# K and V loads of an attention kernel: 16 KB read descriptors over four partitions instead of one 4 KB read per partition

## The chip, the cores and the metric

The kernel runs on one core of a Trainium2 chip. The metric is the device time of one execution in microseconds (us), as the median of several runs; less is better.

The engines' names are those of the profile: PE is TensorE, DVE is VectorE, ACT is ScalarE, POOL is GpSimd and SP is SyncE. PEld is PE's loading of weights, which overlaps its matmuls.

## The reference

```python
B, Hq, Hkv, Sq, Sk, D = 16, 32, 8, 16, 2048, 128        # bf16 throughout

def reference(q, k, v):
    rep = Hq // Hkv                                     # 4 query heads share a K and a V head
    k = jnp.repeat(k, rep, axis=1)
    v = jnp.repeat(v, rep, axis=1)
    scores = jnp.einsum("bhqd,bhkd->bhqk", q, k) * D ** -0.5
    p = softmax(scores, axis=-1)
    return jnp.einsum("bhqk,bhkd->bhqd", p, v)
```

This is grouped-query attention with few queries and long keys: for each of the 128 pairs of batch and K/V head, 64 query rows (4 heads of 16) meet 2,048 keys of 128 numbers. K and V are 64 MiB each and are read once; q and the output are 2 MiB each.

## The kernel before

**Work and tiles.** A group `g` is one of the 128 pairs of batch and K/V head; two groups make a pair `p`, and there are 64 pairs. One K group is 2,048 rows of 256 bytes, 512 KB in one contiguous piece of memory. It is loaded into a tile `Kn` of 128 partitions, where partition `a` holds the 16 consecutive rows 16a to 16a + 15, 4,096 bytes. V goes into `Vb` in the same form. There are 12 buffers of `Kn` (`NBK`) and 16 of `Vb` (`NBV`).

**Steps of a pair.** PE transposes both K tiles, 128 x 128 at a time, into a staging area in PSUM with three banks (`KT`, line 501); DVE or ACT copies each bank to the tile `KT` (lines 565 and 595). PE multiplies it with the transposed queries to get the scores (`S`, line 513, 8 matmuls with 512 columns). DVE scales and negates them and takes the row minimum (`max`, line 575), ACT takes the exponential with the row sums (`exp`, line 601). PE transposes the result (`PT`, line 529), DVE or ACT copies that too, and PE multiplies it with V (`PV`, line 544, 32 matmuls). DVE divides by the row sums (`recip`, `norm`, lines 569 and 586) into the tile `O`, which is stored.

**Who decides the order.** When the program is built, `build_schedule` lays every operation of PE, DVE, ACT and SP out in time with a table of durations and a model of the DMA rate (`_BW`, `_BW_SLOW`, `_RING_MB`). It fixes the order on each engine and which of DVE and ACT does each copy. On the chip the engines follow these orders and meet at semaphores. The order of SP is a list written by `sp_program`: for step `t` the two K loads of pair `t`, a transposing load of 512 query rows every fourth step (`issue_q`, line 438), the two V loads of pair `t - 3`, and the store of pair `t - 7` (line 462).

**The loads.** All transfers are issued by SP on one hardware queue. A K load (`issue_k`, line 447) first waits until PE has transposed the tile that was in the buffer; a V load (`issue_v`, line 455) waits for the `PV` of the pair that used the buffer. Each is one `dma_start` whose source is seen as 128 rows of 2,048 numbers, so it reads 4,096 bytes for each partition and writes 4,096 bytes to it, on 16 DMA engines. Its semaphore counts 16 when all have landed.

Of the kernel before, what the change touches and what calls it, by code (L numbers as in the profile page):

```python
# [18 lines left out]
DSTORE = 7  # L19
QCH = 512  # L20
QLEAD = 6


_DUR = {
# [14 lines left out]

def sp_program(NP, qch_pairs, dv=DV, dstore=DSTORE, qlead=QLEAD):  # L40
    sp = []
    n_qch = (NP + qch_pairs - 1) // qch_pairs
    q_step = {c: max(0, c * qch_pairs - qlead) for c in range(n_qch)}
    for t in range(NP + max(dv, dstore) + 1):
        if t < NP:
            sp += [("K", 2 * t), ("K", 2 * t + 1)]
        for c in range(n_qch):
            if q_step[c] == t:
                sp.append(("Q", c))
        if 0 <= t - dv < NP:  # L50
            sp += [("V", 2 * (t - dv)), ("V", 2 * (t - dv) + 1)]
        if 0 <= t - dstore < NP:
            sp.append(("ST", t - dstore))
    return sp
# [235 lines left out]
def bass_standalone__gqa_softmax__sampling_kernel(  # L290
# [13 lines left out]
    J = Sk // 128  # L304
# [16 lines left out]
    Kn = [sb(f"Kn{i}", [128, J, 128], BF16) for i in range(NBK)]  # L321
    Vb = [sb(f"Vb{i}", [128, J, 128], BF16) for i in range(NBV)]
# [14 lines left out]
    sem_k = [sem(f"sem_k{i}") for i in range(NBK)]  # L337
    sem_v = [sem(f"sem_v{i}") for i in range(NBV)]
# [17 lines left out]
    for op in pe_prog:  # L356
        if op[0] == "KT":
            _, p, gg = op
            for h in range(2):
                ld = dict(kind="KT", pair=p, gg=gg, half=h, u=len(loads), eng=None, eidx=None)  # L360
                ld["bank"] = ld["u"] % NSTAGE
                loads.append(ld)
                kt_loads[(p, gg, h)] = ld
        elif op[0] == "PT":
            _, p = op
            for h in range(2):
                ld = dict(kind="PT", pair=p, gg=None, half=h, u=len(loads), eng=None, eidx=None)
                ld["bank"] = ld["u"] % NSTAGE
                loads.append(ld)
                pt_loads[(p, h)] = ld  # L370
# [30 lines left out]
    def norm_wait(p):  # L401
        eng, n = norm_idx[p]
        return sem_nm[eng], n
# [17 lines left out]
    def bh(g):  # L421
        return divmod(g, Hkv)
# [4 lines left out]
    with nc.Block() as block:  # L427

        @block.gpsimd
        def _(gp):  # L430
            gp.iota(iota_t[:, :], [[1, 128]], base=0, channel_multiplier=-1).then_inc(sem_id, 1)  # L431
            gp.wait_ge(sem_id, 1)
            gp.tensor_scalar(ident[:, :], iota_t[:, :], 0.0, None, op0=ALU.is_equal).then_inc(sem_id, 1)  # L433

        @block.sync
        def _(sp):
            def issue_q(c):
                sp.dma_start_transpose(QT[:, qch * c:qch * (c + 1)], qf[qch * c:qch * (c + 1), :]).then_inc(sem_q[c], 16)

            def issue_k(g):  # L440
                s = g % NBK
                if g >= NBK:
                    gprev = g - NBK
                    ld = kt_loads[(gprev // 2, gprev % 2, 1)]
                    sp.wait_ge(sem_stage, ld["u"] + 1)
                b, h = bh(g)
                sp.dma_start(Kn[s][:, :, :], k[b, h].rearrange("(a j) d -> a j d", j=J)).then_inc(sem_k[s], 16)

            def issue_v(g):
                s = g % NBV  # L450
                if g >= NBV:
                    gprev = g - NBV
                    sp.wait_ge(sem_pv, gprev // 2 + 1)
                b, h = bh(g)
                sp.dma_start(Vb[s][:, :, :], v[b, h].rearrange("(a j) d -> a j d", j=J)).then_inc(sem_v[s], 16)

            ocnt = [0] * NBO

            def issue_store(p):
                s = p % NBO  # L460
                sp.wait_ge(*norm_wait(p))
                sp.dma_start(of[128 * p:128 * (p + 1), :], Osb[s][:, :]).then_inc(sem_o[s], 16)
                ocnt[s] += 1

            for op in sp_prog:
                kind, x = op
                if kind == "K":
                    issue_k(x)
                elif kind == "V":
                    issue_v(x)  # L470
                elif kind == "Q":
                    issue_q(x)
                else:
                    issue_store(x)
            for s in range(NBO):
                if ocnt[s]:
                    sp.wait_ge(sem_o[s], 16 * ocnt[s])

        @block.tensor
        def _(pe):  # L480
# [8 lines left out]
            for op in pe_prog:  # L489
                if op[0] == "KT":  # L490
                    _, p, gg = op
                    lds = [kt_loads[(p, gg, h)] for h in range(2)]
                    g = grp(p, gg)
# [148 lines left out]
```

## Time and profile before

| | |
|---|---|
| median of 3 runs | 373.71 us (373.55 to 373.78) |
| the profiled execution: its own time is the span that the profile gives | 370.2 us |
| the median above the span | 3.5 us |
| busy: PE, PEld, DVE, ACT | 331.0, 260.2, 323.0, 261.9 us |
| mean granted PE clock | 0.995 of full speed |
| read from memory, written | 134.22 MB, 2.10 MB |
| mean rate over all DMA packets | 376 GB/s |
| K and V loads, median from issue to landing | 12.9 us |

Busy time is what an engine spent in instructions, and one engine's work overlaps another's. "Issue to landing" contains the time in the queue behind earlier loads. In a list of waits, "A <- B: us, times, longest" says that instruction group A stood still until B was done; "issue" there means that the engine waited for nothing that the profile shows. In the chain of work that ended last, each row has its start, its length and what it was. In the DMA row, each digit stands for a fortieth of the span and gives the busy share in tenths (9 is 90% or more).

### The profile page before, as it was taken

Reading aid. Unit: us, or ns where it says so; the run is one execution under the profiler, and the core shown is the slowest. Engines: PE = TensorE matmul, PEld = TensorE weight load, DVE = VectorE, ACT = ScalarE, POOL = GpSimd, SP = SyncE. Lnnn points to the kernel's source line nnn. Section 1 sums busy time; section 2 is a strip of 40 time slices with the busy share of each in tenths; the row PEclk is TensorE's granted clock in tenths of the full one; section 3 lists DMA queues with packets and bytes.
Section 4 is the critical chain, followed back from the end, with each engine's and each line's share of the span. In section 5 each row is a group of like instructions: output and inputs, shape, how many; then the busy total and the mean of one; then the engine's idle time right before and its main releaser. Section 6 shows DMA issues by size and latency. Waiting matters only on the chain.

```text
span 370.2 us, 13021 instructions
## 1 busy us (share of the span) xinstructions
PE 331.0 (89%) x5632; PEld 260.2 (70%) x5632; DVE 323.0 (87%) x500; ACT 261.9 (71%) x269; POOL 1.0 (0%) x6
## 2 busy tenths in 40 slices
PE   4698998998998989999898999989999898999995
PEld 3576876776776767677776777777777676776764
DVE  2589998998998989899898998989899897999984
ACT  1267766895666885867878676795867778679593
POOL 1000000000000000000000000000000000000000
PEclk9899999999999999999999999999999999999999
DMA  7999999999999999999999999999999999999993
GB/s 262 375 408 341 408 352 405 405 345 407 352 407 410 342 408 350 406 409 347 410 347 408 400 350 413 348 410 370 380 410 346 408 350 399 409 410 410 406 410 112
DMA packets 54840, 139.26 MB, mean 376 GB/s; under 512 B 22016, under 2 KB 22016, under 8 KB 54784
## 3 DMA queue, kind: packets, MB, share of 16 engines
q1 hardware_dynamic: 54784, 138.43, 102.3%
q8 instruction: 45, 0.74, 0.8%
q14 instruction: 11, 0.09, 0.1%
HBM read 134.22 MB, written 2.10 MB: 368 GB/s over the span
## 4 chain that ended last, share of the span: by engine, by line
PE 68%; ACT 21%; issue 4%; DMA 4%; DVE 3%
PE ST_ps L501 26%; PE S_ps L513 17%; PE O_ps L544 14%; PE ST_ps L529 11%; ACT KT L595 11%; ACT PT L595 8%; DMA Vb<-in_v_dram 3%; DVE Sneg L575 2%; ACT P L601 1%; DMA Kn<-in_k_dram 1%; DVE KT L565 1%; DVE PT L565 0%; DVE O L586 0%; DVE rrec L569 0%
## 5 line engine op out<-in xcount | busy, mean ns | idle before, releaser
L575 DVE TENSOR_SCALAR_CACHE_REDUCE Sneg<-S_ps 128x2048 f32<-128x2048 f32 x64 | 146.7, 2292 | 18.6 <-PE S_ps L513 15.1
L501 PE MATMUL ST_ps<-ident,Kn 128*128 128x128 bf16 x2048 | 143.6, 223 | 18.6 <-ACT KT L595 8.1
L501 PEld LDWEIGHTS ST_ps<-ident,Kn 128*128 128x128 bf16 x2048 | 119.6, 99 | 45.1 <-issue 26.7
L601 ACT ACTIVATE P<-Sneg,nbias 128x2048 bf16<-128x2048 f32 x64 | 128.3, 2005 | 11.5 <-DVE Sneg L575 11.5
L565 DVE COPY KT<-ST_ps 128x1024 bf16<-128x1024 bf16 x177 | 116.3, 683 | 9.8 <-PE ST_ps L501 7.6
L595 ACT ACTIVATE KT<-ST_ps 128x1024 bf16<-128x1024 bf16 x79 | 77.6, 1022 | 48.4 <-PE ST_ps L501 48.3
L595 ACT ACTIVATE PT<-ST_ps 128x1024 bf16<-128x1024 bf16 x59 | 57.2, 1021 | 42.2 <-PE ST_ps L529 42.2
L529 PE MATMUL ST_ps<-ident,P 128*128 128x128 bf16 x1024 | 71.6, 220 | 7.5 <-ACT KT L595 3.8
L529 PEld LDWEIGHTS ST_ps<-ident,P 128*128 128x128 bf16 x1024 | 58.2, 98 | 25.1 <-issue 11.4
L513 PE MATMUL S_ps<-KT,QT 128*64 128x512 bf16 x512 | 68.4, 388 | 6.6 <-ACT KT L595 4.4
L544 PE MATMUL O_ps<-Vb,PT 128*64 128x128 bf16 x2048 | 69.6, 220 | 4.2 <-issue 1.4
L544 PEld LDWEIGHTS O_ps<-Vb,PT 128*64 128x64 bf16 x2048 | 59.1, 110 | 11.1 <-issue 2.5
L565 DVE COPY PT<-ST_ps 128x1024 bf16<-128x1024 bf16 x69 | 44.3, 683 | 3.4 <-PE ST_ps L529 3.2
L513 PEld LDWEIGHTS S_ps<-KT,QT 128*64 128x64 bf16 x512 | 25.3, 109 | 26.3 <-issue 9.9
L586 DVE TENSOR_SCALAR O<-O_ps,rrec 128x128 bf16<-128x128 f32 x62 | 21.5, 346 | 9.1 <-PE O_ps L544 9.1
L569 DVE RECIPROCAL rrec<-rowsum 128x1 f32<-128x1 f32 x64 | 10.2, 159 | 4.3 <-ACT P L601 4.1
L601 ACT ACTIVATION_READ_ACCUMULATOR P<-Sneg,nbias 128x1 f32 x64 | 12.9, 202 | 0.0
L575 DVE DVE_READ_ACCUMULATOR Sneg<-S_ps 128x1 f32 x64 | 5.3, 83 | 0.0
L601 ACT ACT_TABLE_LOAD x1 | 1.3, 1283 | 0.7 <-PEq L627 0.7
L612 ACT ACTIVATE O<-O_ps,rrec 128x128 bf16<-128x128 f32 x2 | 0.7, 368 | 0.4 <-PE O_ps L544 0.4
L433 POOL TENSOR_SCALAR ident<-iota_t 128x128 bf16<-128x128 int32 x1 | 0.5, 536 | 0.1
L431 POOL IOTA iota_t<- 128x128 int32 x1 | 0.2, 235 | 0.4 <-POOLq L627 0.4
(4 smaller groups left out, 0.4 us busy)
## 6 DMA issues: line engine op xcount, KB each, us to landing
Kn<-in_k_dram SPq DMA_DIRECT2D x128, 512.0 KB, 12.9
Vb<-in_v_dram SPq DMA_DIRECT2D x128, 512.0 KB, 12.9
out_dram<-O SPq DMA_DIRECT2D x64, 32.0 KB, 12.6
QT<-in_q_dram SPq DMA_TRANSPOSE x16, 12.3
```

The lines of the kernel that those rows point to most:

```text
L433: gp.tensor_scalar(ident[:, :], iota_t[:, :], 0.0, None, op0=ALU.is_equal).then_inc(sem_id, 1)
L501: ins = pe.transpose(stage_ap(ld["bank"], t), Kn[s][:, j, :], ident[:, :])
L513: ins = pe.matmul(S_ps[64 * gg:64 * (gg + 1), 512 * c:512 * (c + 1)], QT[:, 128 * p + 64 * gg:128 * p + 64 * (gg + 1)], kt[:, gg, 4 * c:4 ...
L529: ins = pe.transpose(stage_ap(ld["bank"], t), P[p % 2][:, 128 * j:128 * (j + 1)], ident[:, :])
L544: ins = pe.matmul(O_ps[64 * gg:64 * (gg + 1), 0:128], pt[:, j, 64 * gg:64 * (gg + 1)], Vb[g % NBV][:, j, :], start=(j == 0), stop=(j == J ...
L565: dve.tensor_copy(evac_dst(ld), stage_bank_ap(ld["bank"])).then_inc(sem_ev["dve"], 1)
L569: dve.reciprocal(rrec[:, p:p + 1], rowsum[:, p:p + 1]).then_inc(sem_rec, 1)
L575: dve.tensor_scalar(Sneg[kk % 2][:, :], S_ps[:, :], -scale, None, op0=ALU.mult, op1=ALU.min, accum_out=nbias[:, kk:kk + 1],).then_inc(sem_ ...
L586: dve.tensor_scalar(Osb[s_][:, :], O_ps[:, 0:128], rrec[:, p:p + 1], None, op0=ALU.mult).then_inc(sem_nm["dve"], 1)
L595: act.activation(evac_dst(ld), stage_bank_ap(ld["bank"]), ACT.Copy).then_inc(sem_ev["act"], 1)
L601: act.activation(P[kk % 2][:, :], Sneg[kk % 2][:, :], ACT.Exp, bias=nbias[:, kk:kk + 1], scale=-1.0, accum_out=rowsum[:, kk:kk + 1],).then ...
L612: act.activation(Osb[s_][:, :], O_ps[:, 0:128], ACT.Copy, scale=rrec[:, p:p + 1]).then_inc(sem_nm["act"], 1)
```

## The change

Each K and V load is issued through a new function, `load_wide`. It builds the copy instruction by hand, with a source of 32 rows of 16,384 bytes and a destination of 128 partitions of 4,096 bytes. Read in order, both sides run through the same 512 KB, so each read fills four neighbouring partitions with the bytes that they had before. Waits, semaphores, the queue, the order on SP, and all instructions of the other engines stay as they were; so do the planner's numbers, and the loads of q and the stores.

```diff
+NREAD = 32
...
+            def load_wide(dst, src, sem_):
+                n = src.size()
+                read = bass.AP(src.tensor, src.offset, [[n // NREAD, NREAD], [1, n // NREAD]])
+                ins = mybir.InstDMACopy(
+                    name=nc.get_next_instruction_name(), engine=sp.engine, queue="qSPDynamicHW",
+                    ins=[sp.lower_ap_dma(read)[0]],
+                    outs=[sp.lower_ap_dma(dst.rearrange("a j d -> a (j d)"))[0]],
+                    mode="Copy",
+                )
+                sp.add_instruction(ins).then_inc(sem_, 16)
...
-                sp.dma_start(Kn[s][:, :, :], k[b, h].rearrange("(a j) d -> a j d", j=J)).then_inc(sem_k[s], 16)
+                load_wide(Kn[s][:, :, :], k[b, h], sem_k[s])
...
-                sp.dma_start(Vb[s][:, :, :], v[b, h].rearrange("(a j) d -> a j d", j=J)).then_inc(sem_v[s], 16)
+                load_wide(Vb[s][:, :, :], v[b, h], sem_v[s])
```

## The prediction

> **What bounds the kernel now.** I read the page first (sections 1 to 3), then the waits of TensorE (PE), then the chain in order of time, then the DMA packet and landing records, which the views only summarise.
>
> ```profile
> span 370.2 us, 13021 instructions
> PE 331.0 (89%) x5632; PEld 260.2 (70%) x5632; DVE 323.0 (87%) x500; ACT 261.9 (71%) x269; POOL 1.0 (0%) x6
> DMA  7999999999999999999999999999999999999993
> q1 hardware_dynamic: 54784, 138.43, 102.3%
> ```
>
> The reader sees two full resources: PE at 89% (VectorE, DVE, at 87%) and DMA engines that never rest until the loads end. Which one sets the end is told by who waits for whom:
>
> ```profile
> PE ST_ps L501 <- ACT KT L595: 8.1, 27, 0.4
> ...
> PE ST_ps L501 <- DMA Kn<-in_k_dram: 4.5, 1, 4.5
> ...
> PE O_ps L544 <- issue: 1.4, 1, 1.4
> PE O_ps L544 <- DMA Vb<-in_v_dram: 1.0, 1, 1.0
> ```
>
> PE waited for a load twice only: 4.5 us for the first K tile, 1.0 us for one V tile. The rest is compute handing work around in an order that the program fixed. The chain in order of time shows the beat and that one late V:
>
> ```profile
> 0.72 3.61 DMA Kn<-in_k_dram
> 4.47 3.59 PE ST_ps L501 x32
> ...
> 59.16 1.36 issue
> ...
> 108.71 1.76 ACT PT L595 x2
> ...
> 130.75 1.76 ACT PT L595 x2
> ...
> 152.86 1.76 ACT PT L595 x2
> ...
> 285.35 1.76 ACT PT L595 x2
> ```
>
> Compute repeats every 22.08 us for four pairs ((285.35 - 108.71)/8). Loads do not: the last landing of V 55, 63, 71, 79 and 87 (eight tiles, four pairs apart) is at 172.0, 194.8, 217.5, 240.2 and 263.0 us, a beat of 22.75 us. So DMA is 3% slower than compute, and lives on a stock built early. The spare time between a tile's last landing and its first use shrinks accordingly: V 39 4.85 us, V 55 4.55, V 71 3.21, V 87 1.91, V 103 0.22 (at 310 us, the tile that PE waited for); K 114 has 0.44 at 322 us. After the last Q transpose (292 us) the loads catch up again, to 2.54 us for the last V. The stock lasts almost exactly as long as the kernel: compute sets the end, loads are next in line by a fraction of a us.
>
> **The change, part by part.**
>
> 1. Reads. 256 loads of 512 KB: per load 128 reads of 4,096 B become 32 of 16,384 B; the 128 writes of 4,096 B stay. Per DMA engine (16 of them) that is 256 x 8 = 2,048 reads before and 512 after, 1,536 fewer. In the packet records a 256 B packet takes 18 ns, a 4,096 B one 159 ns (medians; 32,768 of them), and the shortest 8,192 B ones 309 ns. The first two give (159 - 18)/3,840 = 0.0367 ns per byte plus 8.6 ns per packet, and this line puts 8,192 B at 309.4 ns, which fits. If the 8.6 ns belong to the read, a 16,384 B read takes 610 ns instead of 4 x 159 = 636, and the saving is 1,536 x 8.6 ns = 13.2 us of DMA time over the run, 4%. The other ends: if the 8.6 ns belong to the write, the saving is 0. And a far row: the 45 packets of 16,384 B that are in the trace (instruction fetches) take 1,072 ns, 1.7 times 636. I do not take that row, because one of them took 991 ns at 364 us, when the load queue was done: its destination sets it, and K and V do not go there. I take the 610, nearest to the 8,192 B row, and keep 0 for the range; the far row gets only a small chance.
>
> The Trainium skill, "DMA: Bandwidth & Descriptors", section "Why small descriptors are slow (HBM only)", gives a fixed overhead of about 3 cycles per packet; at that page's 850 MHz that is an estimate of 3.5 ns, and the saving would be 5.4 us in place of 13.2, 0.34 us per beat. That would leave the DMA beat at 22.41 us, still above compute's, but the stock would last, and the sum below would be the same.
>
> 2. What that saving is worth. Almost nothing of it reaches the end. At 4% the K and V part of the DMA beat (16 loads x 8 packets x 159 ns = 20.35 us for four pairs) falls by 0.83 us, so the DMA beat goes from 22.75 to about 21.9 us, under compute's 22.08. Then no tile is late, and what remains is compute's fixed order. Gained: the stall at 310 us. PE stood 1.00 us there, but only part moved on: two beats of 22.08 put the ACT copy at 291.07 us to 313.15, and it is at 313.61; the copy at 302.16 us to 324.24, and it stands at 324.69. So 0.46 us of delay went into the chain, and 0.46 us is the gain. What was hidden by it: the next late thing is ScalarE (ACT), already PE's releaser in the first row of the waits.
>
> 3. The first tiles. PE starts at 4.47 us, 0.14 after K 0 has landed, and K 1 follows at 5.6 us against a use at 6.0. K 0's first packets take 1.09 us, then each engine moves 8 packets. With two reads of 610 ns in place of eight of 159 the landing is 0.05 us earlier; if a row is written only when its whole 16 KB read is in, it is 610 - 159 = 0.45 us later. I take -0.05, and +0.45 for the range.
>
> 4. Issue. SyncE still issues 256 loads in the same order with the same waits; an unobstructed one takes 0.39 to 0.45 us, longer ones wait for room. A beat holds 16 loads, 4 stores and one Q transpose: 16 x 0.45 + 4 x 0.43 + 4.5 = 13.4 us of 22.08, so an issue could take 0.5 us longer before SyncE became the pace. Fewer reads to describe should not lengthen it. Cost: 0.
>
> 5. Engines. PE, DVE and ACT instructions are unchanged in kind and order: 0.
>
> 6. Instruction fetch shares these engines. PE's program comes in 45 fetches of 16 KB. Three PE pauses (0.59 us before 37.08 us, 0.56 before 51.76, 1.36 before 60.52) sit at multiples of 256 instructions, each 1.4 to 1.5 us after a fetch's packet ended; all three are on the chain. A fetch goes ahead of or behind load packets. Nearest rows: it could gain if the engines idle now and then, at most those 2.5 us; it could lose if it must wait for a 16 KB read rather than a 4 KB one. I take 0, since the bytes ahead of it need not change; the losing side is rival 2.
>
> Sum: 0.46 + 0.05 = 0.51 us less. The profiled execution's own time is its 370.2 us span, and the runs' median of 373.71 us lies 3.5 us above it (work around the span, and the difference between executions). I carry that 3.5 over unchanged: 373.71 - 0.51 = 373.2 us.
>
> **The rivals.**
>
> Rival 1, the change does not speed up the DMA: the write side, still 4,096 B a piece, sets the 159 ns. For it: only writes to SBUF partitions are split here, and the records do not tell which side owns the 8.6 ns. Against it: nothing in the trace. Time 373.7 us (373.3 to 374.2 with the first tile's bounds).
>
> Rival 2, slower: PE's instruction fetch waits behind longer reads. Place: the boundaries every 256 PE instructions. The packet of a fetch now ends between 0.67 and 5.5 us before PE needs it, and PE needs about 1.45 us. Eight fetches have 1.46 us or less, five more less than 1.92. If each fetch comes 610 - 159 = 0.45 us later, the eight cost 0.45 each and the five the rest, 1.2 together: 4.9 us, of which stretches where ACT paces may hide half: 376.2 to 378.6 us. It decides from a delay of about 0.3 us on. For it: the pauses on the chain now. Against it: 44 of 45 fetches end at least 1.1 us ahead although the engines are always full. The Trainium skill, same page, section "SWDGE vs HWDGE vs iDMA", prefers packets up to 4,096 B because a packet is where an engine switches between queues; that speaks against 16 KB reads, and no row here shows how long a fetch would wait behind one.
>
> Rival 3, slower: a 16 KB read that fills four rows moves its bytes more slowly, for instance because the next read is not started before four writes are out. There is no stock to pay from: each 1% on the K and V packets is 3.0 us by 322 us (325.6 us x 322/350 x 1%), less the 0.2 to 0.4 us that is spare. 2 to 4% gives 379 to 385 us; the far row of step 1 would give over 500. For it: no row with unequal sides exists. Against it: the straight line through 8,192 B, and that each engine already takes four neighbouring rows, so the memory is read in the same order.
>
> **How the numbers follow.** The forecast (DMA faster, compute sets the end) 0.55, rival 1 0.17, rival 2 0.13, rival 3 0.15. The forecast's own range is 371.6 to 373.8 us: down to 1.6 us more gain if the early fetch pauses shrink, up to the first-tile bound. The range of 8 in 10 goes from 371.6 to 378.6 us: it takes in rivals 1 and 2 and leaves out rival 3 and a little at the low end. About 0.2% (0.75 us) is what a measurement of this kernel can tell from no change. The forecast itself sits at 0.14%, inside that: half of it falls below 372.96 us, with the early pauses or the first tiles helping. Faster 0.27, same 0.43, slower 0.30.
>
> **What would show it.** Right: packets of 16,384 B near 610 ns or a load's GB/s above 410 in slices without a Q transpose; a DMA row with slices under 9 after the first quarter; the 1.0 us wait of L544 for Vb gone; the PE, DVE and ACT busy sums and the 22.08 us beat unchanged. Wrong: rows "PE ... <- DMA Vb" or "<- DMA Kn" of several us (rival 3); many "issue" waits of PE, at multiples of 256 instructions (rival 2); DMA tenths and the wait at 310 us as before (rival 1). A beat shorter than 22.08 us would show that I took for compute's own order what was load pacing.

## The result and the profile after

The changed kernel takes 375.72 us (median of 4 runs, 375.04 to 376.34) against 373.63 us for the kernel before, run beside it. The ratio is 1.0056 by the medians; the recorded comparison of the runs puts it at 1.007, with a 95% interval of 1.0045 to 1.0095. It is slower by about 2 us, where the forecast was 0.5 us faster. The ratios here and below leave out runs more than 1.5% above the fastest of their kernel (two of ten in e16, one of four in e12, one of twelve in e17), while the medians keep them.

The page of the changed kernel, sections 1 to 3:

```profile
span 374.3 us, 13021 instructions
...
PE 330.1 (88%) x5632; PEld 259.4 (69%) x5632; DVE 322.9 (86%) x500; ACT 261.9 (70%) x269; POOL 1.0 (0%) x6
...
DMA  8999999999999999999999999999999999999991
...
DMA packets 30264, 139.26 MB, mean 372 GB/s; under 512 B 22016, under 2 KB 22016, under 8 KB 22016
...
q1 hardware_dynamic: 30208, 138.43, 100.1%
```

The engines' busy sums are those of before within 1 us, so no engine does more. The change does what it says: the 32,768 packets of 4 KB are gone. But the DMA row is as full as it was, and the mean rate is 372 GB/s where before had this:

```profile
DMA packets 54840, 139.26 MB, mean 376 GB/s; under 512 B 22016, under 2 KB 22016, under 8 KB 54784
```

The DMA did not get faster.

The waits of PE in the same run (waiter, released by, us in total, times, longest):

```profile
PE ST_ps L513 <- ACT KT L607: 8.1, 27, 0.4
...
PE ST_ps L513 <- DMA Kn<-in_k_dram: 4.8, 1, 4.8
...
PE ST_ps L513 <- issue: 2.7, 3, 1.2
PE S_ps L525 <- issue: 2.4, 3, 1.3
PE O_ps L556 <- issue: 1.6, 1, 1.6
...
PE ST_ps L541 <- issue: 0.8, 1, 0.8
```

The 1.0 us wait for V is gone. What grew is "issue": 7.5 us in 8 waits. Before had 2.7 us in 4, the 1.4 us at line 544 and these:

```profile
PE S_ps L513 <- issue: 0.7, 2, 0.6
PE ST_ps L501 <- issue: 0.6, 1, 0.6
```

The chain in order of time shows the first K tile later and four of the pauses:

```profile
0.73 3.98 DMA Kn<-in_k_dram
...
35.48 1.06 issue
...
58.89 1.63 issue
...
106.25 1.17 issue
...
286.72 1.35 issue
```

PE's weight loads of the two traces can be set side by side, one by one, since their order is the same. The difference (after less before) starts at +0.37 us, is -0.67 us at 16 us and -1.0 us at 25 us, and then rises in steps to +4.07 us: +0.46 (37 us), +0.27 (52), +0.27 (61), +0.19 (68), +1.10 (106), +0.72 (261), +0.26 (277), +1.94 (284), +0.73 (308). Some 0.9 us come back on the way, 0.6 of them at 310 us, where before waited for V. (The two traced executions lie 4.1 us apart; the medians lie 2.1 us apart.) Each step is at an instruction whose number in PE's queue is 193 modulo 256, within a few: where PE goes over to the next 16 KB of its program. At the pauses, the fetch of that piece had ended 1.3 to 1.5 us earlier.

### The profile page after: what moved, and what is told of

It reads as the page before. It is cut to its first block, busy times and chain, and to the rows that moved or that the text cites. A ratio compares the mean times of both kernels' runs of the same rounds, so it can differ in the third digit from the quotient of the medians.

```text
span 374.3 us, 13021 instructions
## 1 busy us (share of the span) xinstructions
PE 330.1 (88%) x5632; PEld 259.4 (69%) x5632; DVE 322.9 (86%) x500; ACT 261.9 (70%) x269; POOL 1.0 (0%) x6
## 4 chain that ended last, share of the span: by engine, by line
PE 69%; ACT 21%; issue 5%; DVE 3%; DMA 1%
PE ST_ps L513 26%; PE S_ps L525 17%; PE O_ps L556 14%; PE ST_ps L541 12%; ACT KT L607 11%; ACT PT L607 9%; DVE Sneg L587 2%; ACT P L613 1%; DMA Kn<-in_k_dram 1%; DVE KT L577 1%; DVE PT L577 0%; DVE O L598 0%
## 5 line engine op out<-in xcount | busy, mean ns | idle before, releaser
L513 PEld LDWEIGHTS ST_ps<-ident,Kn 128*128 128x128 bf16 x2048 | 118.3, 99 | 47.4 <-issue 28.9
L581 DVE RECIPROCAL rrec<-rowsum 128x1 f32<-128x1 f32 x64 | 10.1, 158 | 4.3 <-ACT P L613 4.1
```

Of the source, the lines that this page charges most:

```text
L513: ins = pe.transpose(stage_ap(ld["bank"], t), Kn[s][:, j, :], ident[:, :])
L581: dve.reciprocal(rrec[:, p:p + 1], rowsum[:, p:p + 1]).then_inc(sem_rec, 1)
```

## The experiments

**How the traces are read here.** Three numbers are taken from the packet records and the instructions of each trace. The *wait* of a fetch is the time from PE's crossing of one 256-instruction boundary to the start of the next fetch (44 per run). PE runs through 256 instructions in about 7.5 us, a fetch takes 1.07 us, and PE went on 1.3 to 1.5 us after it, so a wait above about 5 us makes PE pause at the next boundary. A *meeting* is a fetch that takes 2.5 to 2.6 us in place of 1.07 while a Q transpose comes through. And PE's excess over e4, which has neither late fetches nor late tiles (span 366.7 us), is split into what arises in the first 30 us, what arises at fetch boundaries, and the rest, which is mostly late tiles.

**The hand-built copy and the size of the read.** Three kernels differ from the changed one in one number:

```diff
-NREAD = 32
+NREAD = 128        # e1: 4 KB reads;  64 in e2: 8 KB;  16 in e9: 32 KB
```

> The new load function with 128 reads of 4,096 B, so only the hand-built copy instruction is left of the change. Theory A (a fetch of PE's program stands longer behind 16 KB reads) and theory B (a fetch is late only where a Q transpose runs in front of it, and the change moved the Q transposes) both expect the time of before, 373.6 us within 0.5, with PE pauses of kind issue of 2.7 us in sum as in before. Rival C (the hand-built instruction itself is slower to issue or lands later) expects 375 to 376 us as after.

> 64 reads of 8,192 B, each filling two partitions. Theory A expects a third of the loss: 374.0 to 374.8 us, and fetch waits between those of before (3.9 us on average from the crossing of a 256-instruction boundary to the fetch's start) and after (4.1 us). Theory B expects no order by size: anything from 372 to 377 us, with the pauses where a Q transpose lies between crossing and fetch.

> The change with 16 reads of 32 KB per load, each over eight rows (where the two sides of a copy are dealt differently to the engines, rows come to lie in other partitions; then only its time counts). Theory A (fetch waits grow with the read's size): median wait above 4.2 us (3.6 for 4 and 8 KB, 3.9 for 16 KB), late fetches worth 9 us or more, and a time of 376 us or above. Theory B (only where the transposes fall against the fetches counts): median wait 3.9 us or less, and any time from 372 to 377 us.

e1 took 374.28 us against 372.74 (ratio 1.004, interval 1.0023 to 1.0058): a miss of both theories, and short of the 375 to 376 us of rival C. An issue of a load took 0.60 us against 0.43 before (lower quartiles, which leave out the issues that wait for room), but the trace puts the loss elsewhere: one meeting at 31.6 us, after which the last V landed at 366.9 us (364.3 before), and 4.4 us of waits for V:

```profile
PE O_ps L556 <- DMA Vb<-in_v_dram: 4.4, 8, 1.7
PE S_ps L525 <- issue: 0.2, 1, 0.2
```

There were almost no late fetches. e2 took 372.7 us, ratio 1.0005 (0.999 to 1.002): no change, where theory A wanted a third of the loss; its median wait is 3.60 us, that of 4 KB. This pair leaves a rival standing. All seven runs of e1 lie between 373.5 and 374.6 us, so the copy built by hand, without any 16 KB read, already shows 1.5 of the 2.1 us. e2, built in the same way and with the same issue time (0.59 us), shows none. What the copy built by hand adds is thus not told apart from what the size of the reads adds.

e9 took 630.23 us, ratio 1.686 (1.677 to 1.696), far more than anyone expected, and for another reason:

```profile
span 630.3 us, 13021 instructions
...
DMA  9999999999999999999999999999999999999995
...
DMA packets 26168, 139.26 MB, mean 221 GB/s; under 512 B 22016, under 2 KB 22016, under 8 KB 22016
```

Here the DMA engines themselves are slow: 221 GB/s. A 32 KB packet took 2,346 ns (median), 3.7 times a 16 KB one, and already 2,159 ns among the first two loads. So the cost per byte, which is the same from 4 to 16 KB, nearly doubles at 32 KB. The fetch waits (6.1 us) say nothing about theory A, since the whole stream was slow.

**How deep the load queue is.** With 16 KB reads there were 10.1 loads in flight on average, before 8.4. Two kernels limit that:

```diff
+                if kind in ("K", "V"):
+                    if len(recent) >= DEPTH:
+                        sp.wait_ge(*recent[-DEPTH])
+                    recent.append(...)      # the load's semaphore and its count
```

> The change, and SyncE waits before each load until the load issued eight before it has landed, so at most 8 loads are in flight (10.1 on average after, 8.4 before). Theory A expects 375.7 us as after within 0.7, since the reads stay at 16 KB. Theory B in its narrow form (a deeper queue moved the Q transposes) expects the pauses to return to those of before, and 373.2 us within 0.5. The DMA rate per beat should stay at 22.7 us for four pairs.

> Before, with at most 4 loads in flight (8.4 on average before). If a fetch waits for what the engines have already taken from the load queue, a shorter queue shortens the wait only if it is shorter than what an engine takes ahead; with 4 loads (32 packets of an engine, 5.1 us) theories A and B expect the median wait to fall below 3.3 us, the pauses to below 2 us, and 371.5 us within 1. Rival: the DMA engines run dry between loads, PE waits for tiles, and the time goes above 376 us.

e3 (16 KB reads, 8 in flight) took 375.19 us, ratio 1.0072 (1.0044 to 1.0101): with the shorter queue the loss stays, so the depth is not the cause. e12 (4 KB reads, 4 in flight) took 394.22 us, ratio 1.056 (1.051 to 1.061): the wait of a fetch fell to 3.04 us, as expected, but PE then waited 27 us for tiles, 4.4 of them for the first. The rival was right: the stream needs more than four loads.

**No load traffic.**

```diff
+                if (kind == "K" and x >= NBK) or (kind == "V" and x >= NBV):
+                    continue
```

> The kernel before, with each K and V buffer loaded only once (28 loads of 256; later groups compute on stale tiles, so this leaves out 228 loads). Q transposes and stores stay. Theories A and B both expect that with idle DMA engines the fetches come within 3 us of the crossing, that PE's issue pauses above 0.5 us after the first 40 us are gone, that the 1.0 us wait for V is gone, and a time of 370.5 us within 0.8 (373.6 less 2.5 less 0.5). Rival: the pauses belong to PE's own sequencer and stay at 2.7 us in sum with a time of 373.2 us.

368.31 us, ratio 0.9883 (0.9862 to 0.9904), 2 us less than expected. These are all its PE waits for DMA or issue:

```profile
PE ST_ps L503 <- DMA Kn<-in_k_dram: 4.5, 1, 4.5
PE S_ps L515 <- issue: 0.2, 1, 0.2
```

With idle DMA engines the median wait of a fetch is 0.53 us instead of 3.66. PE's own sequencer is acquitted: without the load traffic the pauses are gone, so they come from fetches that wait for the DMA engines.

**No Q transposes.** The 15 later ones are replaced by plain loads of the same form:

```diff
+                if c > 0:
+                    ...
+                    sp.dma_start(X[:, :, :], k[b, h].rearrange("(a j) d -> a j d", j=J)).then_inc(sem_x, 16)
+                    return          # e7: load_wide(X[:, :, :], k[b, h], sem_x)
```

> Before, with 15 of the 16 Q transposes replaced by a plain 512 KB load of the same 4 KB form into a spare tile (all pairs use the first 512 query rows, so the result is that of other queries). Theory B: with no transpose to meet, no PE pause above 0.5 us at a boundary, fetch waits of 3.7 us on average at most. Theory A says the same of this one; it is the base for the 16 KB form. Time 369 to 372 us by both.

> The same without transposes, all loads with 16 KB reads. Theory A: fetch waits longer than in the 4 KB form by 0.2 to 0.5 us on average, several boundaries late, and a time 1.5 us or more above it. Theory B: waits equal within 0.15 us and times equal within 0.7 us.

e6 took 368.72 us and e7 368.42 us (ratios 0.9875, 0.9854 to 0.9896, and 0.988, 0.9854 to 0.9906): equal within the noise. The median waits were 3.28 and 3.65 us. So theory A's longer wait is there, 0.37 us, but without transposes it costs nothing in three of e7's four runs (368.35 to 368.47 us); each theory missed one half. The fourth (370.36 us) is the one with the trace; two fetches were late there, in the first 60 us, with no transpose in front of them:

```profile
PE ST_ps L525 <- DMA Kn<-in_k_dram: 5.1, 2, 4.8
PE S_ps L537 <- issue: 1.3, 2, 1.1
PE O_ps L568 <- issue: 0.3, 1, 0.3
```

So a transpose is not needed for a late fetch. Leaving the transposes out also gives the loads room: the last V landed at 361.4 us in e6, against 364.3 before.

**The change again, and the fetches shifted.** Empty waits in PE's queue move the boundaries:

```diff
+            for _ in range(48):             # two waits to an instruction: 24 (60 in e8)
+                pe.wait_ge(sem_id, 1)
             pe.wait_ge(sem_id, 2)
```

> The changed kernel once more, beside more runs of before on the same chip, since both vary by about 1 us from run to run. Theory A (each fetch of PE's program waits longer behind 16 KB reads): 2 to 3 us above before in every round, and a second trace with late fetches at other places but again about 9 us of pauses at 256-instruction boundaries. Theory B (only the meeting of a fetch with a Q transpose costs, and it is chance): the excess spreads from 0 to 4 us from run to run.

> After, with 60 empty wait instructions ahead of PE's first work, while PE waits for the first K tile: every 256-instruction boundary falls 60 instructions (about 1.8 us) earlier in the work. Both theories expect the pauses at the shifted boundaries, phase 253 in place of 193 modulo 256, which shows that they are fetches. Theory B: the set of late fetches changes, and the time moves by 1 us or more either way from after. Theory A: other places but the same sum, 375.7 us within 0.8.

> Before, with 24 empty wait instructions ahead of PE's first work (2.7 us by e8's rate of 0.11 us each, just inside the wait for the first K tile). The fetch boundaries move by 24 instructions. Theory B: the late fetches change, and so does the time by up to 2 us either way from 373.2 us. Theory A: pauses stay near 3.7 us in sum and the time within 0.8 us of before.

> After, with the same 24 empty waits. Theory A: still 1.5 us or more above the shifted kernel of before, with a sum of fetch pauses 2 us or more above its. Theory B: within 1 us of it, or below it.

> Before, with the fetch boundaries 44 instructions earlier: 24 empty waits ahead of PE's first work and 20 in the pause before the first transposes of P, which may cost up to 0.5 us there. Theories A and D: within 1 us of before. Theory B: up to 2.5 us from it either way.

> After, with the same shift. Theories A and D: 1.5 to 3.5 us above the shifted kernel of before, as at shift 0 (2.1) and 24 (3.3). Theory B: as often below it as above.

e5: 375.21 us, ratio 1.0056 (1.0035 to 1.0078); its trace is of the one run at 372.73, with 6.0 us at boundaries. e8: 377.36 us, ratio 1.0104 (1.0073 to 1.0135), of which 2.8 us are my own: each empty wait took 0.11 us, 60 did not fit ahead of the first tile, and PE started at 7.66 us in place of 4.84. That leaves about 374.6 us, 1.0 us above before and a little under theory A's range. The pauses moved as they should if they are fetches. They stood before PE's matmuls 339, 586 and 709; in e8 they stand before 680, 1790 and 2160, and counted with the empty instructions these are again 193 modulo 256 (the expectation had the sum the wrong way round).

| instructions shifted | 4 KB reads | 16 KB reads |
|---|---|---|
| 0 | 373.63 | 375.72 |
| 24 | 372.85 (1.0002, 0.9973 to 1.0031) | 376.11 (1.0081, 1.0053 to 1.0108) |
| 44 | 373.63 (1.0001, 0.9982 to 1.0020) | 375.20 (1.0031, 0.9995 to 1.0066) |

(Medians in us; in brackets the ratio to before and its interval.) By the medians the 16 KB form is above the 4 KB form at each shift, by 2.1, 3.3 and 1.6 us. At shifts 0 and 24 that is clear of the noise; at 44 it is not, since e16's runs scatter from 372.1 to 378.2 us and its interval takes in 1. That speaks against theory B, chance alone, but does not rule it out. Where the time goes changes, too. In e11 no fetch makes PE pause, and PE waits for tiles instead:

```profile
PE O_ps L558 <- DMA Vb<-in_v_dram: 6.2, 7, 2.4
PE ST_ps L515 <- DMA Kn<-in_k_dram: 5.8, 5, 4.7
PE S_ps L527 <- issue: 0.2, 1, 0.2
```

Its trace has two meetings, at 167.7 and 192.0 us, and the last V landed at 367.9 us.

**The same dose near to and far from the transposes.**

```diff
+                nread = NREAD if (pos in near) == NEAR else 128
```

> 16 KB reads only for the 113 loads that are issued next to a Q transpose (five before, three after each); the other 143 read 4 KB. Theory A (every fetch waits longer behind 16 KB reads, everywhere): somewhat under half of the loss, 0.7 to 1.3 us above before. Theory D (the loss is made where a 16 KB read, a Q transpose and a fetch meet): nearly the whole loss, 1.8 to 2.6 us above before. Theory B (chance): no relation, 0 to 1.5 us.

> The reverse: 4 KB reads for the 113 loads next to a Q transpose, 16 KB for the other 143. Theory A: somewhat over half of the loss, 1.0 to 1.6 us above before. Theory D: 0.5 us above before at most. Theory B: no relation.

e13 (16 KB reads beside the transposes): 375.2 us, ratio 1.0034 (1.0006 to 1.0061). e14 (16 KB elsewhere): 373.8 us, ratio 1.0011 (0.999 to 1.0031). That leans to theory D: the fewer near reads cost more. The intervals overlap, so it is not settled, and e14's trace does not fit theory D well: it has a meeting at 77.0 us, with 4 KB reads around it, and issue waits of 3.9 us against 2.7 before. e13's runs fall into two groups, four from 372.4 to 372.9 us and eight from 374.7 to 376.6; its trace, of one of the eight, has a meeting at 258.8 us, at the same place as that of the changed kernel's first trace.

**Fewer transposes.**

```diff
-QCH = 512
+QCH = 1024
```

> Before, with 8 transposing loads of 1,024 query rows in place of 16 of 512 (the planner lays out the order anew, so the beat of compute may change). If transposes are the condition: half the stops of the load stream (1.43 us each, 7 fewer after the start, so about 10 us of spare DMA time), half the chances of a meeting, and 368 to 371.5 us. Rival: a transpose of twice the rows stops the stream twice as long and the time stays at 373.4 us within 1.

> After, with the same 8 transposing loads. If the loss needs a transpose: at most 1 us above the 4 KB form with 8 transposes. Rival (16 KB reads cost by themselves): 2 us or more above it.

e17 took 376.81 us, ratio 1.0074 (1.0045 to 1.0104), e18 378.05 us, ratio 1.0124 (1.0089 to 1.016). A miss, and no test: the planner laid out another order, in which compute is slower.

```profile
PE O_ps L544 <- ACT PT L595: 13.0, 40, 1.6
PE ST_ps L501 <- ACT PT L595: 11.7, 49, 0.4
```

e17's PE waits 13.0 us for ACT's copies of P where before had none of that kind, and its last V lands at 353.5 us of 375.5. e18 is 1.2 us above e17 by the medians, between what the two sides expected. No kernel that does the whole work is faster than the one before by more than the noise.

**What the traces say together.**

| trace | read | median wait | start, boundaries, rest over e4 | meetings | last V landed |
|---|---|---|---|---|---|
| before | 4 KB | 3.66 | -0.4, 3.7, 0.3 | 0 | 364.3 |
| e2 | 8 KB | 3.60 | 1.1, 3.0, 0.1 | 0 | 364.9 |
| e15 | 4 KB, shift 44 | 3.62 | -1.8, 1.1, 4.6 | 0 | 365.0 |
| e1 | 4 KB | 3.53 | -0.4, 0.9, 5.3 | 1 (32 us) | 366.9 |
| e10 | 4 KB, shift 24 | 3.59 | -0.5, 1.8, 6.0 | 2 | 368.5 |
| after | 16 KB | 3.94 | -1.4, 9.4, -0.4 | 1 (259 us) | 366.6 |
| e5 | 16 KB | 3.96 | -1.5, 6.0, -0.2 | 1 (32 us) | 365.0 |
| e3 | 16 KB, 8 deep | 3.77 | -0.1, 4.6, -0.4 | 0 | 364.4 |
| e11 | 16 KB, shift 24 | 3.91 | -1.5, 0.3, 8.5 | 2 | 367.9 |
| e16 | 16 KB, shift 44 | 3.95 | -1.1, 1.7, 4.9 | 1 (191 us) | 366.7 |

The median waits do not overlap: 3.53 to 3.66 us for 4 and 8 KB, 3.77 to 3.96 us for 16 KB. At a meeting a transpose comes about 1.5 us late (24.2 to 24.3 us after the last one instead of 22.7, or 21.3 to 21.4 instead of 19.9 at 32 us), so the stream has lost 1.5 us; in e5 and e14 the next one comes as much sooner, and the loss is made good. The two 16 KB traces with the least loss are of the fastest run of their kernel (e5 at 372.73, e3 at 372.58 us), and e10's trace is of its slowest run (376.14 us). Over all runs, 19 of 98 of the kernel before are above 374 us, 4 of 20 of e10 and e15, and 25 of 30 of the kernels with 16 KB reads in this table, but also 6 of 7 of e1.

## Why the prediction was wrong, step by step

**Step 1, the reads: the step that failed first.** The 610 ns do occur: 16 KB packets took 611 ns while the first loads started up. In the full stream the median is 635 ns, which is 4 x 159 = 636. The 8.6 ns per packet that I fitted could be saved only where nothing else held the packet up. The beat of the loads shows it: seven beats, from transpose to transpose, take from 77.34 to 236.25 us after (22.70 us each) and from 76.45 to 235.52 us before (22.72). That saves 0.02 us per beat, not 0.83, which is rival 1's premise (0.17), though not its time. The overhead per packet that the Trainium skill states ("DMA: Bandwidth & Descriptors", "Why small descriptors are slow (HBM only)") gave an estimate of 5.4 us over the run; the beats show 0.3 us, so neither that saving nor mine appeared in this stream.

**Step 2, the 0.46 us for the late V.** The wait is gone in the changed kernel's first trace, but not for the reason given: PE had lost 4.7 us by then, and the loads had that much more time. In e11, where PE was on time, PE waited 6.2 us for V. The reading of the profile stands: compute and loads are within a few us of each other, and what is won on one side is met by the other.

**Step 3, the first tile.** K 0 landed 0.38 us later (4.71 against 4.33 us), near the +0.45 of the bound and not at the -0.05 that I took. The reason given for the bound is not shown: with the old loads K 0 landed at 4.2 to 4.4 us in every trace, with the copy built by hand at 4.5 to 4.7, and e1 with its 4 KB reads (4.55 us) is among these. It did not count: by 16 us PE was 0.67 us ahead.

**Step 4, issue.** Taken as free; the issue of a load went from 0.43 us to 0.59 us (lower quartiles), and SyncE was still not the pace. The term holds as time. e1, with the same longer issue, lost 1.5 us and e2 lost nothing, so whether the issue matters for where fetches and transposes meet is open.

**Step 6, the fetches: where the traced run lost its time.** I took 0, "since the bytes ahead of it need not change". With 16 KB reads the fetches start 0.1 to 0.4 us later, by the medians of the traces. That is rival 2 (0.13), with about 0.3 us where I had 0.45 (its sum, 8 x 0.45 + 1.2, is 4.8 us and not 4.9). Its place was right in the changed kernel's first trace: boundaries 5.7 us above before, less 1.0 us won at the start and 0.7 us by tiles, is about the 4.1 us between the spans. The preference for packets up to 4,096 B that the Trainium skill states ("DMA: Bandwidth & Descriptors", "SWDGE vs HWDGE vs iDMA") agrees in direction with the longer waits at 16 KB (3.77 to 3.96 us), but 8 KB reads (e2) had no longer wait than 4 KB ones (3.60 us). What rival 2 lacked is the transposes. In three of e7's four runs the longer wait by itself cost nothing. With transposes, a fetch that has one in front of it waited about 5 us (median 4.8 before and 5.3 after; the others 3.5 and 3.6), and one that meets it takes 2.6 us and delays all loads. In e11 and e16 the loss came as late tiles and not as pauses at the boundaries, which rival 2 did not foresee either.

**The numbers.** The range of 371.6 to 378.6 us held the time. It held because the range was stretched to take in rival 2, not because of the forecast, whose own range ended at 373.8 us. The sign did not hold: I gave faster and same 0.70 together. The median of before moved by up to 0.9 us between sessions, which is more than the gain I forecast.

**Left open.** That the changed kernel is slower is shown at shifts 0 and 24, and not clear of the noise at 44. That the size of the reads alone makes it so is not shown: the copy built by hand came with every 16 KB read, and with 4 KB reads (e1, shift 0 only) it lost 1.5 us without a longer wait of the fetches. That the medians are equal without transposes is shown at one shift (e6, e7, shift 0), where the loads also had more room. Why some 0.3 us more wait should make meetings and late fetches more frequent is not shown: e13 and e14 lean to the reads beside a transpose, with overlapping intervals, and the traces are one per kernel.

## What to carry to other kernels

Before fewer, longer DMA descriptors are credited with a gain, time one packet of each size in the full stream: if four short ones take as long as one long one, as here (4 x 159 against 635 ns), the descriptor is not the limit. In this kernel PE's program was fetched in competition with the data (a median wait of 3.7 us with the loads, 0.5 us without), so what fills the DMA engines is on PE's path: look for "issue" waits at multiples of 256 instructions and for what runs on the engines just then. When a change swaps the instruction as well as the shape, run the new instruction with the old shape (e1) at every shift, too. In a kernel balanced to 1%, compare executions over several shifts of the program before a difference of a few us is given a cause.

## What the runs showed of the hardware that was not expected

- A Q transpose all but stops the load stream. In the trace of before (at 76.4 us, for one), load packets started at about a fifth of their usual rate for some 1.2 us and then not at all for 0.5 us, and those that were held up took 1.4 us longer (about 1.6 us in place of 0.16).
- Reads of 32 KB that fill eight rows run at 221 GB/s, 16 KB ones that fill four at the rate of 4 KB ones (372 against 376 GB/s over the packets). No run shows why.
- PE's first matmuls ran at about half speed, and that ended earlier after than before: the first 8 matmuls of the scores took 1.92 us from 8.92 us on before, and 1.05 us from 9.11 us on after. That is where the 0.67 us at the start came from; why is open.
- A fetch of 16 KB for PE waits 0.5 us when the DMA engines are nearly idle (e4) and 3.7 us when they are full (before).
